# A chain of three products on one core: wider column blocks in the second product, and the norm's scale inside the hi/lo split of w_out

## The chip, the core and the metric

The kernel runs on one core of a Trainium2 chip. The core has five engines that run side by side: TensorE (PE, matmuls into PSUM), VectorE (DVE), ScalarE (ACT), GpSimd (POOL) and SyncE (SP, which only issues DMA transfers here). The metric is the device time of one execution in microseconds (us).

## What is computed

Attention with a soft cap, then two feed-forwards, all on 896 tokens. Cut to what matters:

```python
def _attn_ref(q, k, v, cap):          # 2 x 12 heads, 448 tokens, 64 wide
    scores = cap * np.tanh(scale * (q @ k.T) / cap)
    ...                                # softmax, times v
def _moe_ref(x, w_in, w_out, g_ln):    # x 896 x 768, w_in 768 x 1024, w_out 1024 x 768
    h = x @ w_in
    e = np.exp(h - h_max)
    solu = h * (e / (np.sum(e, axis=-1, keepdims=True) + 1e-09))
    ln = (solu - mu) / np.sqrt(var + 1e-06) * g_ln
    return ln @ w_out
def _moe2_ref(x, w_gate, w_val, w_out):  # 768 x 1536, 768 x 1536, 1536 x 768
    g = x @ w_gate
    return (g * (1.0 / (1.0 + np.exp(-g))) * (x @ w_val)) @ w_out
```

The weights of both feed-forwards are float64 in memory.

## The kernel before

**Numbers in two parts.** Every product of the feed-forwards is made of float32r parts: a value is split into hi (a copy in float32r) and lo (the value minus hi), and `mm3` adds three matmuls, hi x hi, hi x lo and lo x hi. A float64 weight comes in as a raw tile (`load64`, two buffers) and is made a float32 by `f32`: ScalarE takes the absolute value of the top words, VectorE clamps, shifts and then merges the sign and the low bits with two scalar_tensor_tensor operations on 512 columns (the "bit operations" below). Then ScalarE writes hi and VectorE lo.

**The stages.** Attention goes through 12 pairs of heads. The first feed-forward then goes through 7 tiles of 128 tokens. `ff1_h(t)` is 36 matmuls of 512 columns into two PSUM tiles and a tail of statistics: a maximum on VectorE, an exponential on ScalarE, sums, and the norm, whose last step (line 390) scales the tile `e_t`, on ScalarE for tiles 4 to 6 and on VectorE before. `ff1_T(t)` transposes `e_t` on PE (8 transposes, tiles `lt`) and splits it into hi and lo columns of l. The columns of the 896 tokens lie in three tiles: lA (384, tiles 0 to 2), lB (256, tiles 3 and 4) and lC (256, tiles 5 and 6, a part of the tile y).

**The second product.** w_out is taken in 6 column tiles of 128, `wo_j`, with three buffers. `load_w_out(j)` (line 417) makes each in two halves of 512 rows, that is 4 row blocks of 128 in each. The norm's g_ln is applied there: four ScalarE copies of 128 columns with a scale from a column of `gt`, in place (line 425), then one ScalarE copy of 512 for hi (line 426) and one VectorE subtraction of 512 for lo (line 427). `ff1_x2(j, ...)` is one column block of one output tile: for each of 8 row blocks the three matmuls of `mm3`, 24 in all, with wo_j as the weights and l as the moving columns. Its result is split into hi and lo again as x2, which the second feed-forward (`ff2_gv`, `ff2_out`) reads.

**What sets the order.** Up to line 541 the engines keep the order of the code. From there on a scheduler places the instructions of each engine by its own estimate of times, from the order of the code in the lists `steps` (lines 563 and 568): h[t], T[t], wo[j] and x2[j][n] are what `ff1_h`, `ff1_T`, `load_w_out` and `ff1_x2` put in. Parts marked as pinned keep the code's order also there: the first steps of `f32` in `load_w_out`. Each engine runs its own instructions strictly in the order in which they then stand.

Of the kernel before, what the change touches and what calls it, by code (L numbers as in the profile page):

```python
# [5 lines left out]
F32 = mybir.dt.float32  # L6
F32R = mybir.dt.float32r
U32 = mybir.dt.uint32
I64 = mybir.dt.int64
AF = mybir.ActivationFunctionType  # L10
ALU = mybir.AluOpType
# [25 lines left out]
class Kernel:  # L37
# [295 lines left out]
    def ff1_h(self, t):  # L333

        nc = self.nc
        st = {}

        def mm(kk):
            def go():
                if kk == 0:  # L340
                    if self.htag == "t":
                        ps = self.ph.tile([128, 2, 512], F32, name=f"h_{t}", tag="t")
                        st["h"] = [ps[:, f] for f in range(2)]
                    else:
                        st["h"] = [self.ph.tile([128, 512], F32, name=f"h_{t}_{f}", tag="m") for f in range(2)]
                a, z = kk == 0, kk == self.KD - 1
                xh, xl = self.xcols(t, kk)
                wh, wl = self.wi
                f = [slice(0, 512), slice(512, 1024)]
                for x, w, s, e in ((xh, wh, a, False), (xh, wl, False, False), (xl, wh, False, z)):  # L350
                    for i in range(2):
                        self.PE.matmul(st["h"][i], x, w[:, kk, f[i]], start=s, stop=e)
                if z:
                    tail()
            return go

        def tail():
            sm = self.slot("sm", [128, 32], f"sm_{t}", F32, bufs=3)
            e = self.slot("e", [128, self.F1], f"e_{t}", F32, bufs=2)
            h = st["h"]  # L360
            for f in range(2):
                self.V.tensor_reduce(sm[:, f:f + 1], h[f], axis=AX.X, op=ALU.max)
            self.V.tensor_scalar(sm[:, 2:3], sm[:, 0:1], sm[:, 1:2], -1.0, op0=ALU.max, op1=ALU.mult)
            for f in range(2):
                self.A.activation(e[:, f * 512:(f + 1) * 512], h[f], AF.Exp, bias=sm[:, 2:3],
                                     accum_out=sm[:, 3 + f:4 + f])
            self.V.tensor_scalar(sm[:, 5:6], sm[:, 3:4], sm[:, 4:5], 1e-9, op0=ALU.add, op1=ALU.add)
            self.V.reciprocal(sm[:, 6:7], sm[:, 5:6])

            sq = t >= 5  # L370
            for f in range(2):
                ef = e[:, f * 512:(f + 1) * 512]
                self.V.scalar_tensor_tensor(ef, ef, sm[:, 6:7], h[f], op0=ALU.mult, op1=ALU.mult,
                                               **({"accum_out": sm[:, 8 + f:9 + f]} if sq else {}))
                if not sq:
                    self.V.bn_stats(sm[:, 8 + 6 * f:14 + 6 * f], ef)
            if sq:
                r = self.F1 ** 0.5
                self.V.tensor_scalar(sm[:, 20:21], sm[:, 8:9], sm[:, 9:10], -1 / (self.F1 * r), op0=ALU.add, op1=ALU.mult)
                for f in range(2):  # L380
                    self.A.activation(h[f], e[:, f * 512:(f + 1) * 512], AF.Square, bias=sm[:, 20:21], scale=1 / r,
                                         accum_out=sm[:, 10 + f:11 + f])
                self.V.tensor_scalar(sm[:, 22:23], sm[:, 10:11], sm[:, 11:12], 1e-6, op0=ALU.add, op1=ALU.add)
            else:
                r = -1.0
                self.V.bn_aggr(sm[:, 20:22], sm[:, 8:20].rearrange("p (a s) -> p a s", s=6))
                self.V.tensor_scalar(sm[:, 22:23], sm[:, 21:22], 1e-6, None, op0=ALU.add)
            self.G.tensor_tensor(sm[:, 23:24], sm[:, 22:23], self.mhalf, op=ALU.pow)
            self.V.tensor_scalar(sm[:, 24:25], sm[:, 20:21], sm[:, 23:24], r, op0=ALU.mult, op1=ALU.mult)
            if t >= 4:  # L390
                self.A.activation(e, e, AF.Identity, bias=sm[:, 24:25], scale=sm[:, 23:24])
            else:
                self.V.tensor_scalar(e, e, sm[:, 23:24], sm[:, 24:25], op0=ALU.mult, op1=ALU.add)
            self.ln[t] = e

        return [(1.3, mm(kk)) for kk in range(self.KD)]
# [20 lines left out]
    def load_w_out(self, j):  # L417

        w = self.wos[j] = self.wo.tile([128, 2, self.K1, 128], F32R, name=f"wo_{j}", tag="wo")
        for i in range(2):  # L420
            c = slice(4 * i, 4 * i + 4)
            src = self.w_out[i * 512:(i + 1) * 512, j * 128:(j + 1) * 128].rearrange("(f p) d -> p f d", p=128)
            f = self.f32(self.load64(src, f"wo_{j}_{i}"), f"wo_{j}_{i}", pin=True).rearrange("p (f d) -> p f d", f=4)
            for m in range(4):
                self.A.activation(f[:, m], f[:, m], AF.Copy, scale=self.gt[:, 4 * i + m:4 * i + m + 1])
            self.hi_act(w[:, 0, c], f)
            self.lo_dve(w[:, 1, c], f, w[:, 0, c])

    def ff1_x2(self, j, get, N, o):

# [75 lines left out]
    def run(self):  # L506
        nc = self.nc
        KD, K1, K2, F1 = self.KD, self.K1, self.K2, self.F1
# [19 lines left out]
        w = [self.w_in_steps(i) for i in range(2 * KD)]  # L528
# [5 lines left out]
        h = [self.ff1_h(t) for t in range(7)]  # L534
# [12 lines left out]

        self.pt = self.ph = self.pool("pm", bufs=8, space=PSUM)
        self.htag, self.ttag = "m", "m"
        lA = self.slot("l", [128, K1, 2, 384], "lA")  # L550
        T = [self.ff1_T(t, lambda: lA, 128 * t) for t in range(3)]
        lp = self.pool("lp", side="right")
        self.wo = self.pool("wo", bufs=3, side="right")
        lB = lp.tile([128, K1, 2, 256], F32R, name="lB", tag="lB")
        self.y = self.slot("x", [128, KD * 2 * 896], "y")
        lC = self.y[:, :4096].rearrange("p (f u n) -> p f u n", f=K1, u=2)
        T3, T4 = self.ff1_T(3, lambda: lB, 0), self.ff1_T(4, lambda: lB, 128)
        T5, T6 = self.ff1_T(5, lambda: lC, 0), self.ff1_T(6, lambda: lC, 128)
        wo = [[(0.0, lambda j=j: self.load_w_out(j))] for j in range(KD)]
        blocks = ((lambda: lA, 384, 0), (lambda: lB, 256, 384), (lambda: lC, 256, 640))  # L560
        x2 = [[[self.ff1_x2(j, *blocks[n])] for n in range(3)] for j in range(KD)]

        steps = h[1] + T[0] + h[2] + T[1] + h[3][:2] + T[2] + h[3][2:] + h[4][:3] + wo[0] + h[4][3:] + wo[1] + h[5][:5] + T3 + h[5][5:] + h[6][:2] + T4 + h[6][2:]
        for _, f in steps:
            f()
        X = [self.slot(f"wi{u}", [128, 6144], f"x2_{u}") for u in range(2)]
        self.x2 = [X[j // 3][:, j % 3 * 1792:(j % 3 + 1) * 1792].rearrange("p (u n) -> p u n", u=2) for j in range(KD)]
        steps = x2[0][0] + x2[0][1] + wo[2] + x2[1][0] + T5 + x2[1][1] + T6 + x2[0][2] + x2[1][2]
        for j in range(2, KD):
            if j + 1 < KD:  # L570
                steps += wo[j + 1]
            if j >= KD - 2:
                steps += [(0.0, lambda i=j - KD + 2: self.load_gv(0, i))]
            steps += x2[j][0] + x2[j][1] + x2[j][2]
        for _, f in steps:
            f()
        self.wo.release()
# [1 line left out]


        ap = self.pool("ap", side="right")
        big = self.slot("l", [128, 6144], "a_0")
        ab = [big] + [ap.tile([128, 5376], F32R, name=f"a_{i}", tag=f"a_{i}") for i in range(1, 4)]
        w2x = self.y[:, :4608].rearrange("p (f u n) -> p f u n", f=6, u=2)
        for fc in range(K2):
            self.a[fc] = ab[fc // 3][:, fc % 3 * 1792:(fc % 3 + 1) * 1792].rearrange("p (u n) -> p u n", u=2)
        for fc in range(6):
            self.w2[0, fc] = w2x[:, fc]
        for i, t in enumerate([big] + X):
            self.w2[0, 6 + i] = t[:, 5376:].rearrange("p (u n) -> p u n", u=2)  # L590
        for fc in range(K2):
            for i, (N, o) in enumerate(((384, 0), (512, 384))):
                if fc + 1 < K2:
# [57 lines left out]
```

## Time and profile before

| | us |
|---|---|
| median of 3 runs | 509.64 (509.06 to 510.04) |
| the profiled execution | 509.66 |
| its span, first to last instruction | 507.9 |
| PE busy | 496.3 |
| VectorE busy | 348.0 |
| ScalarE busy | 256.7 |
| GpSimd busy | 20.7 |

The profiled execution's time is its span and some 1.8 us around it. A row of a timeline gives the start, the length, the engine, what is written and read, and how many instructions follow each other; in brackets stands idle time of the engine before it and what ended that. Lengths of instructions in a row overlap, since each engine begins the next before the last has left it; what one costs in a row is read from start to start.

### The profile page before, as it was taken

The numbers are of one execution on the slowest core, as the hardware profiler recorded it, in microseconds if no ns is written. First come the engines' busy times: TensorE is split into PE (matmuls) and PEld (weight loads), VectorE is DVE, ScalarE is ACT, GpSimd is POOL, SyncE is SP. The second block draws the span as 40 slices with busy tenths as digits, with TensorE's granted clock in tenths as the row PEclk, the third lists the DMA queues.
The fourth block names the chain that finished last, engine by engine and source line by source line (L and its number), as shares of the span: only waits on it lengthen the run. The fifth ranks groups of instructions, "written<-read, shape, count | busy, mean of one in ns | idle before, by whom it ended". The sixth has DMA issues, their size and how long they took to land.

```text
span 507.9 us, 7456 instructions
## 1 busy us (share of the span) xinstructions
PE 496.3 (98%) x2920; PEld 411.3 (81%) x2920; DVE 348.0 (69%) x625; ACT 256.7 (51%) x388; POOL 20.7 (4%) x63
## 2 busy tenths in 40 slices
PE   6999999999999999999999999999999999999996
PEld 5454444446788899999999988889999889999996
DVE  2788888873778895677899999897997868200000
ACT  2999999990313696474545454353444434100000
POOL 1111111110000000000000000000000000000000
PEclk8999999999999999999999999999999999999999
DMA  8955555320000222145354545435243525111111
GB/s 169 218 127 151 132 151 129 91 70 2 0 1 0 82 85 84 43 146 165 125 176 136 185 127 162 149 124 161 98 148 94 168 80 157 31 32 31 32 31 32
DMA packets 66916, 52.40 MB, mean 103 GB/s; under 512 B 35904, under 2 KB 62272, under 8 KB 66880
## 3 DMA queue, kind: packets, MB, share of 16 engines
q1 hardware_dynamic: 65184, 50.90, 35.5%
q10 hardware_dynamic: 1664, 1.02, 0.6%
q8 instruction: 23, 0.38, 0.3%
q14 instruction: 13, 0.11, 0.1%
q0 software_dynamic: 32, 0.00, 0.0%
HBM read 49.16 MB, written 2.75 MB: 102 GB/s over the span
## 4 chain that ended last, share of the span: by engine, by line
PE 93%; DMA 2%; ACT 2%; DVE 2%; issue 0%; ACTq 0%; POOL 0%; POOLq 0%
PE o L29 17%; PE g L29 17%; PE v L29 17%; PE x L29 10%; PE h L29 10%; PE pv L29 8%; PE sc L29 7%; PE S L29 4%; PE T L29 2%; DMA q<-in_q_dram 1%; PE lt L29 1%; DVE sm L29 1%; ACT P L29 1%; ACT wo L29 1%; DMA wo_raw<-in_moe_w_out_dram 1%; DVE e L29 0%
## 5 line engine op out<-in xcount | busy, mean ns | idle before, releaser
L29 PE MATMUL g<-x,y 128*128 128x512 f32 (+1 forms) x432 | 91.3, 363 | 0.0
L29 PE MATMUL v<-x,y 128*128 128x512 f32 (+1 forms) x432 | 90.5, 362 | 0.0
L29 PEld LDWEIGHTS g<-x,y 128*128 128x128 f32 x432 | 78.3, 188 | 8.8
L29 PEld LDWEIGHTS v<-x,y 128*128 128x128 f32 x432 | 78.2, 188 | 8.5
L29 PE MATMUL h<-wi,x 128*128 128x512 f32 x252 | 58.8, 392 | 0.0
L29 PEld LDWEIGHTS h<-wi,x 128*128 128x128 f32 x252 | 46.8, 188 | 10.9 <-issue 1.4
L29 PE MATMUL o<-x,a 128*128 128x384 f32 x294 | 52.4, 336 | 0.0
L29 PEld LDWEIGHTS o<-x,a 128*128 128x128 f32 x294 | 51.2, 188 | 0.0
L29 ACT ACTIVATE P<-sc,c 112x896 f32<-112x896 f32 x48 | 45.6, 999 | 3.1 <-PE sc L29 2.7
L29 ACT ACTIVATE P<-P,cp 112x1792 f32<-112x1792 f32 x24 | 43.1, 1795 | 0.5
L29 PE MATMUL pv<-P,v 112*64 112x448 f32 x192 | 41.2, 551 | 0.0
L29 PEld LDWEIGHTS sc<-ks 64*112 64x112 f32 x288 | 24.1, 176 | 19.6 <-issue 8.5
L493 ACT ACTIVATE ob<-o 128x384 f32<-128x384 f32 x14 | 6.9, 491 | 65.0 <-PE o L29 65.0
L29 PE MATMUL sc<-ks 64*112 64x448 f32 x288 | 36.8, 387 | 1.0 <-ACT P L29 1.0
L29 PE MATMUL o<-y,a 128*128 128x384 f32 x189 | 34.3, 337 | 0.0
L29 PEld LDWEIGHTS o<-y,a 128*128 128x128 f32 x189 | 33.2, 188 | 0.1
L29 PEld LDWEIGHTS pv<-P,v 112*64 112x64 f32 x192 | 11.7, 136 | 23.9 <-issue 16.6
L29 PE MATMUL x<-lA,wo 128*128 128x384 f32 x144 | 28.1, 337 | 0.9 <-ACT wo L29 0.9
L29 PEld LDWEIGHTS x<-lA,wo 128*128 128x128 f32 x144 | 24.3, 188 | 1.1 <-ACT wo L29 1.1
L29 ACT ACTIVATE a<-sg 128x384 fp32r<-128x384 f32 (+1 forms) x24 | 13.9, 578 | 21.9 <-DVE sg L469 21.8
L29 DVE SCALAR_TENSOR_TENSOR w<-w_raw,w 128x768 uint32<-128x768 uint32 (+1 forms) x26 | 23.1, 892 | 0.4
L29 ACT ACTIVATE wv<-wv_raw 128x768 f32<-128x768 f32 x12 | 10.9, 910 | 24.6 <-DMA wv_raw<-in_moe_w_val_dram 24.6
(97 smaller groups left out, 682.5 us busy)
## 6 DMA issues: line engine op xcount, KB each, us to landing
wg_raw<-in_moe_w_gate_dram SPq DMA_DIRECT2D x12, 768.0 KB, 4.3
wv_raw<-in_moe_w_val_dram SPq DMA_DIRECT2D x12, 768.0 KB, 4.3
w_raw<-in_moe_w_out_dram SPq DMA_DIRECT2D x11, 768.0 KB, 4.5
wi_raw<-in_moe_w_in_dram SPq DMA_DIRECT2D x12, 512.0 KB, 4.2
wo_raw<-in_moe_w_out_dram SPq DMA_DIRECT2D x12, 512.0 KB, 3.5
v<-in_v_dram SPq DMA_DIRECT2D x24, 112.0 KB, 2.8
k<-in_k_dram SPq DMA_DIRECT2D x23, 112.0 KB, 4.1
q<-in_q_dram SPq DMA_DIRECT2D x23, 112.0 KB, 4.6
```

The source lines that it names most:

```text
L29: i = f(*a, **k)
L493: nc.scalar.activation(ob, acc, AF.Copy)
```

## The change

Four things change, all from the first feed-forward's second product on.

- The columns of l lie in two tiles instead of three: lA has 512 (tiles 0 to 3), lB 384 (tiles 4 to 6), and lC is gone. `ff1_x2` then has two column blocks for each output tile. The orders of the lists `steps` are written anew: wo[0] to wo[2] stand before the end of the h stage, then come the first blocks of x2[0], x2[1] and x2[2] with T5 and T6 between them.
- In `load_w_out` the in-place scaling goes. ScalarE writes hi of each row block straight from the unscaled float32, with the scale; VectorE writes lo of each row block with one scalar_tensor_tensor of 128 columns, value times scale minus hi.
- The last step of the norm for tiles 4 and 5 is on VectorE instead of ScalarE.
- The tiles of the second feed-forward's a lie in three tiles instead of four.

```diff
-            if t >= 4:
+            if t >= 6:
                 self.A.activation(e, e, AF.Identity, bias=sm[:, 24:25], scale=sm[:, 23:24])
...
             for m in range(4):
-                self.A.activation(f[:, m], f[:, m], AF.Copy, scale=self.gt[:, 4 * i + m:4 * i + m + 1])
-            self.hi_act(w[:, 0, c], f)
-            self.lo_dve(w[:, 1, c], f, w[:, 0, c])
+                g, hi = self.gt[:, 4 * i + m:4 * i + m + 1], w[:, 0, 4 * i + m]
+                self.A.activation(hi, f[:, m], AF.Copy, scale=g)
+                self.V.scalar_tensor_tensor(w[:, 1, 4 * i + m], f[:, m], g, hi.bitcast(F32), op0=ALU.mult, op1=ALU.subtract)
...
-        lA = self.slot("l", [128, K1, 2, 384], "lA")
+        lA = self.slot("l", [128, K1, 2, 512], "lA")
...
-        lB = lp.tile([128, K1, 2, 256], F32R, name="lB", tag="lB")
+        lB = lp.tile([128, K1, 2, 384], F32R, name="lB", tag="lB")
...
-        lC = self.y[:, :4096].rearrange("p (f u n) -> p f u n", f=K1, u=2)
-        T3, T4 = self.ff1_T(3, lambda: lB, 0), self.ff1_T(4, lambda: lB, 128)
-        T5, T6 = self.ff1_T(5, lambda: lC, 0), self.ff1_T(6, lambda: lC, 128)
+        T3, T4 = self.ff1_T(3, lambda: lA, 384), self.ff1_T(4, lambda: lB, 0)
+        T5, T6 = self.ff1_T(5, lambda: lB, 128), self.ff1_T(6, lambda: lB, 256)
...
-        blocks = ((lambda: lA, 384, 0), (lambda: lB, 256, 384), (lambda: lC, 256, 640))
-        x2 = [[[self.ff1_x2(j, *blocks[n])] for n in range(3)] for j in range(KD)]
-
-        steps = h[1] + T[0] + h[2] + T[1] + h[3][:2] + T[2] + h[3][2:] + h[4][:3] + wo[0] + h[4][3:] + wo[1] + h[5][:5] + T3 + h[5][5:] + h[6][:2] + T4 + h[6][2:]
+        blocks = ((lambda: lA, 512, 0), (lambda: lB, 384, 512))
+        x2 = [[[self.ff1_x2(j, *blocks[n])] for n in range(2)] for j in range(KD)]
+
+        steps = h[1] + T[0] + h[2] + T[1] + h[3][:2] + T[2] + h[3][2:] + wo[0] + h[4][:3] + wo[1] + h[4][3:] + h[5][:2] + T3 + h[5][2:] + wo[2] + h[6][:2] + T4 + h[6][2:]
...
-        steps = x2[0][0] + x2[0][1] + wo[2] + x2[1][0] + T5 + x2[1][1] + T6 + x2[0][2] + x2[1][2]
-        for j in range(2, KD):
-            if j + 1 < KD:
-                steps += wo[j + 1]
-            if j >= KD - 2:
-                steps += [(0.0, lambda i=j - KD + 2: self.load_gv(0, i))]
-            steps += x2[j][0] + x2[j][1] + x2[j][2]
+        steps = x2[0][0] + x2[1][0] + T5 + x2[2][0] + T6
+        for j in range(3):
+            steps += x2[j][1] + wo[j + 3]
+        for j in range(3, KD):
+            if j > 3:
+                steps += [(0.0, lambda i=j - 4: self.load_gv(0, i))]
+            steps += x2[j][0] + x2[j][1]
...
-        big = self.slot("l", [128, 6144], "a_0")
-        ab = [big] + [ap.tile([128, 5376], F32R, name=f"a_{i}", tag=f"a_{i}") for i in range(1, 4)]
+        big = self.slot("l", [128, 8192], "a_0")
+        ab = [big] + [ap.tile([128, 7168], F32R, name=f"a_{i}", tag=f"a_{i}") for i in range(1, 3)]
```

On PE, behind the end of the h stage, before. In the names, `x2_1_0` is the PSUM tile of output tile 1 from column 0 on, `lt_5_0` the first transposes of token tile 5; the last number is a running one.

```order
L29 MATMUL lt_4_1_1798<-ident_100,e_4_1661 128x128 x4
L29 MATMUL x2_0_0_1849<-lA_1374,wo_0_1613 128x384 x14
L29 MATMUL x2_0_384_1876<-lB_1381,wo_0_1613 128x256
L29 MATMUL x2_0_0_1849<-lA_1374,wo_0_1613 128x384 x10
L29 MATMUL x2_0_384_1876<-lB_1381,wo_0_1613 128x256 x12
L29 MATMUL x2_1_0_1932<-lA_1374,wo_1_1678 128x384
L29 MATMUL x2_0_384_1876<-lB_1381,wo_0_1613 128x256 x11
L29 MATMUL x2_1_0_1932<-lA_1374,wo_1_1678 128x384 x11
L29 MATMUL lt_5_0_1959<-ident_100,e_5_1760 128x128 x4
```

The same place on PE now, as far as the first matmuls behind tile 6's transposes:

```order
L29 MATMUL lt_4_1_1839<-ident_100,e_4_1698 128x128 x4
L29 MATMUL x2_0_0_1890<-lA_1374,wo_0_1593 128x512 x24
L29 MATMUL x2_1_0_1917<-lA_1374,wo_1_1646 128x512 x5
L29 MATMUL lt_5_0_1944<-ident_100,e_5_1768 128x128 x4
L29 MATMUL lt_5_1_1951<-ident_100,e_5_1768 128x128 x4
L29 MATMUL x2_1_0_1917<-lA_1374,wo_1_1646 128x512 x19
L29 MATMUL x2_2_0_1958<-lA_1374,wo_2_1785 128x512 x2
L29 MATMUL lt_6_0_1985<-ident_100,e_6_1871 128x128 x4
L29 MATMUL lt_6_1_1992<-ident_100,e_6_1871 128x128 x4
L29 MATMUL x2_2_0_1958<-lA_1374,wo_2_1785 128x512 x10
```

Output tile 1 now stands behind the 24 matmuls of one block of output tile 0; before, all but one of its matmuls stood behind both blocks, 48. The second block of tile 0 has moved behind tile 6's transposes.

On VectorE, before, the last rows up to the second bit operation on wo_1's second half (`wo_1_1`; `wo_1_0` is the first half as float32, `sm_t` the statistics of token tile t):

```order
L29 TENSOR_TENSOR wo_1_1678<-wo_1_0_1681,wo_1_1678 128x512
L29 TENSOR_SCALAR sm_6_1829<-sm_6_1829 128x1
L29 TENSOR_SCALAR wo_1_1_1695<-wo_1_1_1695 128x512
L29 TENSOR_SCALAR sm_5_1759<-sm_5_1759 128x1
L29 TENSOR_SCALAR wo_1_1_1695<-wo_1_1_1695 128x512
L29 SCALAR_TENSOR_TENSOR wo_1_1_1695<-wo_1_1_raw_1693,wo_1_1_1695 128x512
L29 TENSOR_SCALAR sm_5_1759<-sm_5_1759 128x1
L29 TENSOR_SCALAR sm_6_1829<-sm_6_1829 128x1
L29 SCALAR_TENSOR_TENSOR wo_1_1_1695<-wo_1_1_raw_1693,wo_1_1_1695 128x512
```

And now, the last 12 of 31 instructions from the first maximum over tile 6's h to the same second bit operation:

```order
L29 SCALAR_TENSOR_TENSOR e_6_1871,sm_6_1870<-e_6_1871,sm_6_1870,h_6_1_1819 128x512
L29 TENSOR_TENSOR x2_0_1888<-x2_0_0_1890,x2_0_1888 128x512
L29 TENSOR_SCALAR wo_2_0_1788<-wo_2_0_1788 128x512
L29 TENSOR_SCALAR wo_1_1_1665<-wo_1_1_1665 128x512
L29 TENSOR_SCALAR sm_6_1870<-sm_6_1870 128x1
L29 TENSOR_TENSOR lB_1381<-lt_5_0_1944,lB_1381 128x4x128
L29 TENSOR_TENSOR lB_1381<-lt_5_1_1951,lB_1381 128x4x128
L29 TENSOR_SCALAR wo_2_0_1788<-wo_2_0_1788 128x512
L29 SCALAR_TENSOR_TENSOR wo_1_1_1665<-wo_1_1_raw_1663,wo_1_1_1665 128x512
L29 TENSOR_SCALAR sm_6_1870<-sm_6_1870 128x1
L29 SCALAR_TENSOR_TENSOR wo_2_0_1788<-wo_2_0_raw_1786,wo_2_0_1788 128x512
L29 SCALAR_TENSOR_TENSOR wo_1_1_1665<-wo_1_1_raw_1663,wo_1_1_1665 128x512
```

The 19 ahead of these are two maxima over h, two bit operations and one one-operand step on wo_1_0, one such step on wo_1_1, two subtractions into lB, four scalar_tensor_tensor of 128 columns into wo_1, tile 5's scaling (128x1024), one step with a sum on e_6, a reciprocal and four single-column steps. The second half of wo_1 now stands behind steps on wo_2 and behind tile 5's columns of lB, which came after it before.

## Rows read from the trace of the kernel before

**Rows 1.** The page, part 1: busy us (share of the span) and instructions by engine.

```profile
PE 496.3 (98%) x2920; PEld 411.3 (81%) x2920; DVE 348.0 (69%) x625; ACT 256.7 (51%) x388; POOL 20.7 (4%) x63
```

**Rows 2.** Stretch: length, busy us of PE, PEld, DVE, ACT, POOL; granted clock; DMA.

```profile
242.20:416.02 173.82, 173.82 (x867) 156.43 (x866) 152.64 (x237) 78.97 (x121) 0.00 (x0) 1.00 0.46 141
```

**Rows 3.** Timeline of PE, matmuls of three widths: start us, us, what.

```profile
222.61 2.25 PE L29 MATMUL x<-lA,wo 128*128 128x384 f32 x12
224.69 1.59 PE L29 MATMUL x<-lB,wo 128*128 128x256 f32 x12
226.12 1.54 PE L29 MATMUL x<-y,wo 128*128 128x256 f32 x12
227.50 0.51 PE L29 MATMUL x<-lA,wo 128*128 128x384 f32 x2
...
262.98 4.28 PE L29 MATMUL g<-x,y 128*128 128x512 f32 x18
267.10 4.24 PE L29 MATMUL v<-x,y 128*128 128x512 f32 x18
```

**Rows 4.** Timeline of PE: end of the h stage, and two waits.

```profile
179.10 1.03 PE L29 MATMUL lt<-ident,e 128*128 128x128 f32 x8
179.89 2.67 PE L29 MATMUL x<-lA,wo 128*128 128x384 f32 x14
...
194.91 1.03 PE L29 MATMUL lt<-ident,e 128*128 128x128 f32 x8
196.32 0.50 PE L29 MATMUL x<-y,wo 128*128 128x256 f32 x2 [0.37 <-ACT y L29]
...
215.41 1.31 PE L29 MATMUL x<-y,wo 128*128 128x256 f32 x10
217.60 0.61 PE L29 MATMUL x<-lA,wo 128*128 128x384 f32 x2 [0.88 <-ACT wo L29]
```

**Rows 5.** Timeline of VectorE behind h[6]: start us, us, what.

```profile
179.21 0.69 DVE L29 TENSOR_REDUCE sm<-h 128x1 f32<-128x512 f32 x1
179.81 0.68 DVE L29 TENSOR_TENSOR wo<-wo,wo 128x512 fp32r<-128x512 f32 x1
...
184.82 0.68 DVE L29 SCALAR_TENSOR_TENSOR wo<-wo_raw,wo 128x512 uint32<-128x512 uint32 x1
```

**Rows 6.** Groups by form, 130 to 245 us: count | busy us, mean ns | idle before.

```profile
L29 DVE SCALAR_TENSOR_TENSOR e<-e,sm,h 128x512 f32<-128x512 f32 x14 | 9.9, 744 | 0.2
...
L29 DVE TENSOR_SCALAR sm<-sm 128x1 f32<-128x1 f32 x28 | 5.4, 200 | 5.6 <-POOL sm L29 2.8 <-ACT e L29 2.6
L29 DVE TENSOR_SCALAR wo<-wo 128x512 f32<-128x512 f32 x12 | 5.1, 424 | 2.1 <-ACT wo L29 1.7
...
L29 DVE TENSOR_TENSOR x<-x,x 128x256 fp32r<-128x256 f32 x12 | 5.1, 422 | 4.2 <-ACT x L29 4.0
...
L29 DVE TENSOR_SCALAR e<-e,sm 128x1024 f32<-128x1024 f32 x4 | 3.3, 813 | 0.1
...
L29 DVE TENSOR_TENSOR lB<-lt,lB 128x512 fp32r<-128x512 f32 x4 | 2.7, 684 | 0.5 <-ACT lB L29 0.5
...
L29 ACT ACTIVATE wo<-wo,gt 128x128 f32<-128x128 f32 x48 | 15.4, 394 | 5.6 <-DVE wo L29 5.6
...
L29 ACT ACTIVATE e<-e,sm 128x1024 f32<-128x1024 f32 x3 | 3.7, 1247 | 3.2 <-DVE sm L29 3.2
```

**Rows 7.** Busy us by stretch, as in rows 2: the span's start and end.

```profile
5.40:7.70 2.30, 0.00 (x0) 0.00 (x0) 0.75 (x4) 0.51 (x1) 0.00 (x0) 1.00 1.14 257
7.80:9.00 1.20, 0.00 (x0) 0.00 (x0) 0.00 (x0) 0.00 (x0) 0.00 (x0) 0.50 1.37 169
9.00:14.50 5.50, 5.44 (x29) 4.24 (x30) 3.20 (x6) 2.42 (x3) 0.45 (x1) 0.50 0.96 206
...
503.90:506.00 2.10, 0.00 (x0) 0.00 (x0) 0.00 (x0) 0.49 (x1) 0.00 (x0) 1.00 0.29 86
506.10:507.90 1.80, 0.00 (x0) 0.00 (x0) 0.00 (x0) 0.00 (x0) 0.00 (x0) 0.50 0.01 3
```

More of the change, by code (lines that the diff above doesn't have):

```diff
@@ L581, in run @@
         ap = self.pool("ap", side="right")
-        big = self.slot("l", [128, 6144], "a_0")
-        ab = [big] + [ap.tile([128, 5376], F32R, name=f"a_{i}", tag=f"a_{i}") for i in range(1, 4)]
+        big = self.slot("l", [128, 8192], "a_0")
+        ab = [big] + [ap.tile([128, 7168], F32R, name=f"a_{i}", tag=f"a_{i}") for i in range(1, 3)]
         w2x = self.y[:, :4608].rearrange("p (f u n) -> p f u n", f=6, u=2)
         for fc in range(K2):
-            self.a[fc] = ab[fc // 3][:, fc % 3 * 1792:(fc % 3 + 1) * 1792].rearrange("p (u n) -> p u n", u=2)
+            self.a[fc] = ab[fc // 4][:, fc % 4 * 1792:(fc % 4 + 1) * 1792].rearrange("p (u n) -> p u n", u=2)
         for fc in range(6):
             self.w2[0, fc] = w2x[:, fc]
-        for i, t in enumerate([big] + X):
-            self.w2[0, 6 + i] = t[:, 5376:].rearrange("p (u n) -> p u n", u=2)
+        for i, t in enumerate([big[:, 7168:7936], X[0][:, 5376:], X[1][:, 5376:]]):
+            self.w2[0, 6 + i] = t.rearrange("p (u n) -> p u n", u=2)
         for fc in range(K2):
```

## The prediction

> **What bounds the kernel now.** I read the page first, then tables of busy time by stretch, then the timelines of PE and VectorE. TensorE is busy for 496.3 of the 507.9 us [rows 1], and in the second feed-forward for every one of 173.82 us [rows 2]. So the time is the length of one row of matmuls: it gets shorter only where a matmul gets cheaper or where PE stops waiting. I therefore ask two things of the change: what the same columns cost in other block widths, and which instruction PE waits for at each place where it may wait, before and after.
>
> **Matmuls in wider blocks.** The second product of the first feed-forward has 6 output tiles of 8 x 3 = 24 matmuls per column block: 432 matmuls in blocks of 384, 256 and 256, and 288 in blocks of 512 and 384. I take the price of one from start to start, since the durations overlap. Twelve of 384 columns take 224.69 - 222.61 = 2.08 us (173 ns each), twelve of 256 from lB 1.43 us (119 ns), twelve of 256 from y 1.38 us (115 ns); eighteen of 512 in the second feed-forward take 267.10 - 262.98 = 4.12 us (229 ns; the v group after them 227) [rows 3]. One of each width: 407 ns before, 400 to 402 ns after, so 144 x 6 or 7 ns: **1.0 us less**, 0.7 to 1.1. The columns are the same; only a fixed part of about 7 ns per matmul goes.
> The Trainium skill, page "TensorE: Matmul & The Clock Gate", section "Back-to-back issue gap", gives an isolated matmul N/2.4 + 2.5 ns. The trace disagrees with it for 512 columns (216 ns by the page, 227 to 229 here). By the page's formula, and this is an estimate, a dropped matmul saves 2.5 ns, the gain would be 0.4 us, and the sums below would each lie 0.6 us higher.
>
> **Waits that go.** PE has two holes in this stage. After the transposes of tile 6 it waits for the high half of lC (in y): 1.41 us from the 8 transposes to the next matmul, where the 8 after tile 4 need 0.79. Before the fourth output tile it waits for wo_3: 2.19 us from the start of 10 matmuls to the next, where 10 need 1.15 [rows 4]. Together 0.62 + 1.04 = **1.66 us**. In the changed order all six blocks of the first three output tiles stand before wo_3 is wanted, and 10 matmuls of x2[2] right behind tile 6's transposes, reading lA, which was full long before. I take both holes as gone.
>
> **The wait that comes.** In the new order PE reaches the second half of wo_1 much sooner in work, and VectorE reaches it much later. Both run from the same moment, the end of h[6].
> PE's side: 8 transposes of tile 4 (0.79 us), 24 matmuls of x2[0], 5 of x2[1], 8 transposes of tile 5 (0.79), 7 more of x2[1]; the thirteenth reads row block 4 of wo_1, from the second half. That is 36 x 0.227 + 2 x 0.79 = 9.8 us. Before, two blocks of x2[0] stood ahead of x2[1], and VectorE began the last bit operation on wo_1 184.82 - 179.10 = 5.7 us after h[6] [rows 4, 5].
> VectorE's side: in the new order 31 instructions stand from the first maximum over tile 6's h to the last bit operation on wo_1's second half. An instruction starts the next one some 0.09 us before its own end (0.69 us long, the next 0.60 us later [rows 5]). By that: 11 of 512 elements at 0.60, the last at its full 0.69; 5 one-operand steps on 512 (0.424 long [rows 6]) at 0.34; two of e with a sum at 0.66; tile 5's scaling of 1024, which came over from ScalarE, at 0.73; 7 single-column steps (0.20 long) at 0.11; and 4 of the new scale-and-subtract on 128 columns. No row shows that operation. Two-operand rows go by 0.131 us per 128 elements (0.422 for 256, 0.684 for 512), which gives 0.29; a scale from a column adds 0.06 (0.744 against 0.684) [rows 6]: 0.35 long, 0.26 apart. From below a single-column step bounds it (0.20 long), from above the 256-wide one with the column (0.48): 0.12 to 0.39 apart. I take 0.26, since both neighbours lie on one line. Sum: 6.60 + 0.69 + 1.70 + 1.32 + 0.73 + 0.77 + 1.04 = 12.9 us, from 0.1 us after h[6] [rows 4, 5]. Then ScalarE must write the high part of the block, 0.39 us [rows 6], before PE may go on: 13.4 us. Tile 6's statistics and the bit operations on wo_2's first half, which stand among these 31, are what was put before wo_1; nothing in the queue is free to wait.
> **PE stands still for 13.4 - 9.8 = 3.6 us**; I take 3.5, and 3.0 to 4.1 by the bounds of the new operation. After that ScalarE gives a row block of wo_1 at least each 0.39 us and PE needs 0.68 for its three matmuls, so there is one wait, not four. Queued behind the waiting matmul on PE is everything.
> Costed at nothing: ScalarE loses 12 copies of 512 and two scalings of 1024; that gives PE nothing while VectorE is the late one. Tile 4's scaling on VectorE is covered by h[6], 36 matmuls of 0.227 us. Tile 5's is the 13th of the 31, some 5.4 us after h[6], and its transposes come after 0.79 + 29 x 0.227 = 7.4 us; without those 2.0 us of cover its 0.73 us would show. From wo_3 on, each tile of w_out is converted behind 24 matmuls of 512 and 24 of 384 (9.6 us), and its VectorE work of 2 x (2 x 0.34 + 2 x 0.60 + 4 x 0.26) = 5.8 us fits. The loads of wo_0 to wo_2 stand earlier in the code, but SP issues the same transfers in the same order, each when its raw buffer has been read. The second feed-forward changes only in where its tiles lie.
> Sum without anything else: -1.0 - 1.66 + 3.5 = +0.84 us.
>
> **What the standstill does to the clock.** TensorE's granted clock is at its upper level (2.4 GHz, 1.00) through the second feed-forward [rows 2]. It fell to the lower (1.2 GHz, 0.50) twice. At the start PE did nothing from 5.4 us at the latest until 9.0; to 7.7 us the clock was 1.00, from 7.8 us it was 0.50, and it stayed there through 5.5 us in which PE worked again [rows 7]. At the end the last matmul ended at 503.9 us, the clock was 1.00 until 506.0 and 0.50 from 506.1 on [rows 7]. So it fell some 2.3 and 2.2 us into an idle stretch, and the new standstill is longer than either. The holes of before, 1.0 us and less, never took it. That it falls here in every execution the two rows don't prove; I give it two chances in three. Its price: at half the rate the work done in the slow stretch takes twice as long, so half of 5.5 us is lost if as much follows as at the start, 2.75 us, and nothing if it doesn't fall. I take **1.6 us**, a little over the middle, since here 512-column matmuls follow at once where at the start short ones and waits did.
> The Trainium skill, the same page, section "Why this matters for your kernels", says to leave no long idle gap between bursts of matmuls, since the clock then goes back to half. By that rule the fall is certain rather than likely, and the sum is that of my forecast.
>
> **The forecast.** The profiled execution took 509.66 us for its span of 507.9, and the median of the runs is 509.64, so changes in the span are added to 509.65. Forecast: 509.65 + 0.84 + 1.6 = **512.1 us**, by itself 511.0 to 513.6.
>
> **The rivals.**
> 1. *The same standstill, and the clock stays up.* For it: two falls are few, and both came beside idle engines. 509.65 + 0.84 = 510.5 us, 510.0 to 511.2 by the new operation's bounds: at the edge of what can be told from no change.
> 2. *The standstill is short, and the wider blocks and closed holes show.* It would need VectorE to finish wo_1 some 2.5 us sooner than its 31 instructions add up to. Against it: in this stretch of before it runs back to back, and their order is fixed. Even then tile 6 is late next: its last statistic stands right behind those 31, and its scaling on ScalarE is 1.25 us long [rows 6], which leaves up to 1 us of waiting. It gives 509.65 - 2.66 + 0 to 1.0 = 507.0 to 508.0; above that it runs into the first rival. It decides in its own favour once the new wait is under 1.6 us.
> 3. *The hole moves on.* wo_2's second half comes late as well, as it is converted behind wo_1: another 1 us or a longer slow stretch, 513.6 and more. Against it: after the standstill PE has two dozen matmuls of x2[1] and x2[2] before it needs that half.
>
> **How the numbers follow.** Forecast 0.52, first rival 0.30, second 0.15, third 0.03. What a measurement of this kernel can tell from no change is about 0.2%, 1.0 us: 508.6 to 510.7. The first rival lies in it for 0.21 of its 0.30 and above it for 0.09; of the second, 0.12 lie below 508.6 and 0.03 inside. Faster 0.12, same 0.24, slower 0.52 + 0.09 + 0.03 = 0.64. The range leaves out the second rival and the third: 509.6 to 513.6.
>
> **What the changed profile would show.** Right: 288 matmuls of x2 at 227 and 173 ns from start to start; no wait on y or wo_3; one PE wait of some 3.5 us in x2[1] at about 189 us, put down to ScalarE's wo with VectorE busy without a hole before it; and behind it a stretch with the granted clock at 0.50. Wrong: a PE wait there under 2 us, or matmuls of 512 columns at more than 235 ns at full clock; the new VectorE operation outside 0.20 to 0.48 us; a wait of over 0.5 us at wo_2 to wo_5; or a clock that stays at 1.00 through the standstill, which turns the forecast into the first rival.

## The result and the profile after

The changed kernel takes **512.59 us** (median of 14 runs, 511.09 to 515.53) against 509.50 for the kernel before on the same chip (14 runs): ratio **1.0069**, 95% interval 1.0054 to 1.0084. The forecast was 512.1 in 509.6 to 513.6. The profiled execution took 512.51 us for a span of 510.7.

The page, part 1, answers to [rows 1]: 1.5 us more of PE busy time with 144 matmuls fewer, and 5.8 us more on VectorE.

```profile
PE 497.8 (97%) x2776; PEld 405.5 (79%) x2776; DVE 353.8 (69%) x657; ACT 246.8 (48%) x368; POOL 21.7 (4%) x63
```

The timeline of PE from tile 4's transposes to the second feed-forward answers to [rows 3, 4]: start us, length, what is written and read, count, and in brackets idle time and what ended it.

```profile
178.18 1.04 PE L29 MATMUL lt<-ident,e 128*128 128x128 f32 x8
178.97 6.90 PE L29 MATMUL x<-lA,wo 128*128 128x512 f32 x29
185.71 1.03 PE L29 MATMUL lt<-ident,e 128*128 128x128 f32 x8
186.50 1.85 PE L29 MATMUL x<-lA,wo 128*128 128x512 f32 x7
191.50 0.73 PE L29 MATMUL x<-lA,wo 128*128 128x512 f32 x2 [3.15 <-ACT wo L29]
192.59 4.62 PE L29 MATMUL x<-lA,wo 128*128 128x512 f32 x12 [0.35 <-DVE wo L29]
197.04 1.03 PE L29 MATMUL lt<-ident,e 128*128 128x128 f32 x8
...
201.21 2.77 PE L29 MATMUL x<-lB,wo 128*128 128x384 f32 x15
203.81 2.46 PE L29 MATMUL x<-lA,wo 128*128 128x512 f32 x10
206.11 9.18 PE L29 MATMUL x<-lB,wo 128*128 128x384 f32 x52
...
244.65 3.31 PE L29 MATMUL g<-x,y 128*128 128x384 f32 x18
```

Read the starts. Tile 4's transposes to the first g: 244.65 - 178.18 = 66.47 us, before 242.20 - 179.10 = 63.10. So **3.4 us come in this stage**. PE does 7 matmuls from 186.50 and is at the next one only at 191.50: 5.00 us where 7 need 1.6. Two matmuls on, it waits once more, this time for VectorE. Then 12 matmuls take 197.04 - 192.59 = 4.45 us, 371 ns each instead of 230: that is the slow clock. The table by stretch (length, busy us and count of PE, PEld, DVE, ACT, POOL, granted clock, DMA share, GB/s) shows it, and the second feed-forward beside it, which answers to [rows 2]:

```profile
193.53:196.94 3.41, 3.41 (x10) 2.60 (x9) 2.48 (x7) 2.21 (x6) 0.00 (x0) 0.50 0.69 206
244.65:418.27 173.62, 173.62 (x865) 156.25 (x865) 151.97 (x236) 78.29 (x121) 0.00 (x0) 1.00 0.45 140
```

The list of PE's waits over this stage has two entries only. None names y, and none wo_3:

```profile
PE x L29 <- ACT wo L29: 3.1, 1, 3.1
PE x L29 <- DVE wo L29: 0.4, 1, 0.4
```

VectorE's timeline behind h[6] answers to [rows 5], and two groups by form to [rows 6]; the second fence gives count, busy us, mean ns of one, idle time before.

```profile
178.15 0.69 DVE L29 TENSOR_REDUCE sm<-h 128x1 f32<-128x512 f32 x1 [0.54 <-PE h L29]
...
182.84 0.81 DVE L29 TENSOR_SCALAR e<-e,sm 128x1024 f32<-128x1024 f32 x1
183.56 0.16 DVE L29 RECIPROCAL sm<-sm 128x1 f32<-128x1 f32 x1
183.63 0.86 DVE L29 SCALAR_TENSOR_TENSOR wo<-wo,gt,wo 128x128 fp32r<-128x128 f32 x3
184.41 0.74 DVE L29 SCALAR_TENSOR_TENSOR e<-e,sm,h 128x512 f32<-128x512 f32 x1
...
189.73 1.28 DVE L29 SCALAR_TENSOR_TENSOR wo<-wo_raw,wo 128x512 uint32<-128x512 uint32 x2
191.46 0.21 DVE L29 TENSOR_SCALAR sm<-sm 128x1 f32<-128x1 f32 x1 [0.44 <-POOL sm L29]
191.59 0.68 DVE L29 SCALAR_TENSOR_TENSOR wo<-wo_raw,wo 128x512 uint32<-128x512 uint32 x1
192.19 1.14 DVE L29 SCALAR_TENSOR_TENSOR wo<-wo,gt,wo 128x128 fp32r<-128x128 f32 x4
```

```profile
L29 ACT ACTIVATE wo<-wo,gt 128x128 fp32r<-128x128 f32 x48 | 15.3, 392 | 8.9 <-DVE wo L29 8.9
L29 DVE SCALAR_TENSOR_TENSOR wo<-wo,gt,wo 128x128 fp32r<-128x128 f32 x48 | 14.4, 347 | 1.4 <-ACT wo L29 1.4
```

From 178.15 to the end of the last bit operation on wo_1 (189.73 + 1.28 = 191.01) VectorE works without a gap. ScalarE's hi row blocks begin at 191.05, having waited for it, and PE goes on at 191.50. ScalarE's timeline:

```profile
191.05 1.28 ACT L29 ACTIVATE wo<-wo,gt 128x128 fp32r<-128x128 f32 x4 [1.93 <-DVE wo L29]
```

The lo row blocks, at 192.19, stand behind a statistic that waits 0.44 us for GpSimd and behind a bit operation on wo_2: this is the second wait.

Outside this stage two things differ. PE is at tile 4's transposes 0.92 us earlier. This comes from the start, which the edit doesn't touch: PE waits 2.19 us for the first q instead of 3.73, and the slow clock there lasts 3.41 us instead of 6.83. And the last 252 matmuls take 0.45 us longer; the timelines of PE, of the kernel before and of the changed one:

```profile
459.84 44.03 PE L29 MATMUL o<-x,a 128*128 128x384 f32 x252
```

```profile
462.24 44.48 PE L29 MATMUL o<-x,a 128*128 128x384 f32 x252
```

3.37 - 0.92 + 0.45 - 0.04 (the gate and value products) = 2.86 us, and the profiled executions differ by 512.51 - 509.66 = 2.85.

### The profile page after: what moved, and what is told of

Read it like the earlier page. It is cut to its first block, busy times and chain, and to the rows that moved or that the text cites. A ratio compares the mean times of both kernels' runs of the same rounds, so it can differ in the third digit from the quotient of the medians.

```text
span 510.7 us, 7184 instructions
## 1 busy us (share of the span) xinstructions
PE 497.8 (97%) x2776; PEld 405.5 (79%) x2776; DVE 353.8 (69%) x657; ACT 246.8 (48%) x368; POOL 21.7 (4%) x63
## 3 DMA queue, kind: packets, MB, share of 16 engines
HBM read 49.16 MB, written 2.75 MB: 102 GB/s over the span
## 4 chain that ended last, share of the span: by engine, by line
PE 92%; DVE 3%; DMA 2%; issue 1%; ACT 0%; POOLq 0%; ACTq 0%; POOL 0%; SPq 0%; DVEq 0%
PE o L29 17%; PE g L29 17%; PE v L29 17%; PE x L29 10%; PE h L29 10%; PE pv L29 8%; PE sc L29 7%; PE S L29 4%; DMA q<-in_q_dram 2%; PE T L29 2%; DVE sm L29 1%; PE lt L29 1%; DVE wo L29 1%; DVE e L29 1%; DVE lB L29 0%
## 5 line engine op out<-in xcount | busy, mean ns | idle before, releaser
L29 PE MATMUL x<-lA,wo 128*128 128x512 f32 x144 | 38.1, 409 | 3.5 <-ACT wo L29 3.1
L29 PEld LDWEIGHTS x<-lA,wo 128*128 128x128 f32 x144 | 27.5, 195 | 9.4 <-ACT wo L29 3.6
L29 PE MATMUL x<-lB,wo 128*128 128x384 f32 x144 | 27.4, 335 | 0.0
L29 PEld LDWEIGHTS x<-lB,wo 128*128 128x128 f32 x144 | 25.4, 188 | 1.2
```

The costliest lines, as they stand in the source:

```text
L29: i = f(*a, **k)
```

## Experiments

**Is the clock really paid for?** My theory: of the loss, some 1.7 us are the slow clock, and the rest is the standstill. The rival: the 512-column matmuls behind the wait are slow for another reason, such as lo row blocks that arrive late. Two kernels keep the changed one and its wait, and give PE useless matmuls of 512 columns into a PSUM tile that nobody reads, 13 or 7 of them, in the place where it would stand. For this x2[1]'s first block is cut in two, and PE keeps the code's order in the second part.

```diff
+                spare = self.pt.tile([128, 512], F32, name="spare", tag="m")
+                for _ in range(n):
+                    self.PE.matmul(spare, w[:, 0, 3, :], l[:, 3, 0, :], start=True, stop=True)
                 for fc in range(4, 8):
```

> The changed kernel with 13 matmuls of 512 columns more on TensorE, into a PSUM tile that nobody reads, placed behind tile 5's transposes and before the second half of x2[1]; VectorE's order up to wo_1 is the changed kernel's. They take 13 x 0.227 = 2.95 of the 3.4 to 3.8 us in which PE stands still, so PE arrives at the same moment but has worked. If the slow clock behind the standstill is due to the standstill: clock at 1.00 behind it, about 1.7 us less than the changed kernel, 510.8 us. If it comes from something else (the 512-column blocks, the load of all engines): no gain, 512.6 us, and half clock at the same place.

> The same with 7 such matmuls (1.6 us), which leaves some 2.0 us of standstill in one piece. Standstill theory: between the two, 510.8 to 512.6 us, with the clock falling in fewer of the executions than in the changed kernel. If the fall has another cause: 512.6 us.

With 13: 510.72 us, ratio 1.0038 (1.0027 to 1.0050), as the first theory has it. PE's timeline, and busy time and granted clock of PE over the stretch:

```profile
178.78 1.03 PE L29 MATMUL lt<-ident,e 128*128 128x128 f32 x8
...
189.93 1.99 PE L29 MATMUL spare<-lA,wo 128*128 128x512 f32 x8
192.10 0.73 PE L29 MATMUL x<-lA,wo 128*128 128x512 f32 x2 [0.18 <-ACT wo L29]
193.18 3.03 PE L29 MATMUL x<-lA,wo 128*128 128x512 f32 x12 [0.35 <-DVE wo L29]
196.05 1.03 PE L29 MATMUL lt<-ident,e 128*128 128x128 f32 x8
...
243.56 3.31 PE L29 MATMUL g<-x,y 128*128 128x384 f32 x18
```

```profile
188.00:204.00 16.00, 15.47 (x78) 1.00 0.33 100
```

The same 12 matmuls now take 2.87 us instead of 4.45 us, though the wait for lo ahead of them is the same 0.35 us; the clock stays at 1.00. The stage is 243.56 - 178.78 = 64.78 us long, 1.69 less than in the changed kernel (66.47), with useless work in the place of the hole. So the clock's price is shown: 1.7 us, half of the slow stretch of 3.41.

With 7: 511.44 us, ratio 1.0052 (1.0037 to 1.0067). In the profiled execution the wait for hi was 1.55 us and that for lo 0.35, the clock fell all the same, again for 3.41 us, and the stage was as long as in the changed kernel (66.45).

```profile
192.92:196.33 3.41, 3.41 (x10) 2.67 (x9) 2.76 (x7) 2.09 (x7) 0.00 (x0) 0.50 0.72 205
```

A profile is one execution, but the mean granted clock of every execution is on record. One of the six with 7 useless matmuls, the one that took 510.48 us, has 1.000: there the clock did not fall at all. The span times one minus the mean clock is 4.0 us on average over the 14 executions of the changed kernel and 2.2 over 50 of the kernel before. The 1.8 us more are what about one such stretch in each execution would give. This is an estimate, and the scatter is wide: the six with 13 and the six with 7 both give 3.0.

**Which part of the change brings the standstill?** Theory: VectorE's row behind h[6], whatever lengthens it. One part is undone at a time, or done alone. Undone alone: the norm of tiles 4 and 5 (`oldnorm`), the new split (`oldsplit`). Done alone: the wide blocks (`blocks`, both of these undone, but with the new orders of the lists and the new places of a), the split (`splitonly`, in the kernel before).

```diff
# oldnorm, in the changed kernel
-            if t >= 6:
+            if t >= 4:
# oldsplit, in the changed kernel; splitonly is its reverse in the kernel before
-                self.A.activation(hi, f[:, m], AF.Copy, scale=g)
-                self.V.scalar_tensor_tensor(w[:, 1, 4 * i + m], f[:, m], g, hi.bitcast(F32), op0=ALU.mult, op1=ALU.subtract)
+                self.A.activation(f[:, m], f[:, m], AF.Copy, scale=self.gt[:, 4 * i + m:4 * i + m + 1])
+            self.hi_act(w[:, 0, c], f)
+            self.lo_dve(w[:, 1, c], f, w[:, 0, c])
```

> The changed kernel with one part undone: the scaling of tiles 4 and 5 is on ScalarE again. 0.73 us less in VectorE's row before wo_1, and the scheduler places wo_1's steps anew: the wait breaks into two of about 1.0 and 1.2 us with one row block between them. Theory of the order: about 1.2 us less waiting than the changed kernel, and the clock stays up in some executions: 509.3 to 511.3 us. Rival, the new split alone is the cause: no more than the 0.7 us of VectorE work, 511.9 us.

> The changed kernel with the w_out split undone: four scaled copies in place, one copy and one subtraction of 512. VectorE does 0.44 us less for each half of a wo tile, ScalarE 0.53 more. If the new 128-column operation is the cause: the standstill shrinks by 0.9 us or more and the time falls to 510 or below. Theory of the order: the scheduler places the rows anew and another wait comes in at wo_2, so it is no better, 511.5 to 513.5 us, with waits of about 2.7 us at x2[1] and 1.3 at x2[2].

> The wider blocks alone: the w_out split and the place of the norm's scaling as before the change. Theory of the order: the blocks bring wo_1 closer to the end of the h stage, and that alone makes the standstill; two waits of about 1.6 and 2.8 us at x2[1], the clock falls, 512.7 to 514.7 us. If the other two parts make it: 507 to 508.5 us.

> The kernel before with only the w_out split changed: blocks of 384, 256 and 256, and the order of the list as they were. If the new split were neutral: 509.5 us. Theory of the order: its 0.44 us more for each half push back tile 5's and tile 6's rows on VectorE, so that PE waits about 2.5 us for each of the two (at tile 5's transposes and for lC); 513 us, and 515 where the clock falls.

| kernel | us | ratio to before (95%) | PE's waits in the stage | clock in the profiled execution |
|---|---|---|---|---|
| changed | 512.59 | 1.0069 (1.0054 to 1.0084) | 3.1 + 0.4 | fell at 193.53 |
| oldnorm | 510.61 | 1.0025 (1.0012 to 1.0038) | 0.8 + 0.9 | fell at 192.08 |
| oldsplit | 511.74 | 1.0054 (1.0037 to 1.0071) | 2.6 | fell at 192.75 |
| blocks | 513.10 | 1.0078 (1.0064 to 1.0092) | 2.4 + 1.3 | stayed at 1.00 |
| splitonly | 512.77 | 1.0070 (1.0053 to 1.0087) | 2.3 + 2.3 | fell at 200.45 |

The stretch of slow clock in `oldnorm`, in the columns of the table by stretch:

```profile
192.08:195.49 3.41, 3.41 (x11) 2.62 (x10) 3.08 (x9) 1.54 (x5) 0.00 (x0) 0.50 0.50 154
```

The lists of PE's waits (us in total, times, longest) of `oldnorm`, `blocks` and `splitonly`:

```profile
PE x L29 <- DVE wo L29: 0.9, 1, 0.9
PE x L29 <- ACT wo L29: 0.8, 1, 0.8
```

```profile
PE x L29 <- ACT wo L29: 3.7, 2, 2.4
```

```profile
PE lt L29 <- ACT e L29: 2.3, 1, 2.3
PE x L29 <- ACT y L29: 2.3, 1, 2.3
```

The blocks with their new order alone cost as much as everything together, and so does the split alone, each by making PE wait for what VectorE and ScalarE have yet to finish, but at different places: wo_1 with the new blocks, tiles 5 and 6 with the old ones. So the parts do not add up. But the theory of VectorE's row alone is too narrow, as `blocks` shows at its longer wait:

```profile
189.45 0.68 DVE L29 SCALAR_TENSOR_TENSOR wo<-wo_raw,wo 128x512 uint32<-128x512 uint32 x1
190.47 1.27 ACT L29 ACTIVATE wo<-wo,gt 128x128 f32<-128x128 f32 x4
191.64 1.24 ACT L29 ACTIVATE e<-e,sm 128x1024 f32<-128x1024 f32 x1
192.77 0.62 ACT L29 ACTIVATE wo<-wo 128x512 fp32r<-128x512 f32 x1
193.44 3.81 PE L29 MATMUL x<-lA,wo 128*128 128x512 f32 x14 [2.39 <-ACT wo L29]
```

VectorE has done its bit operations by 190.13; then ScalarE's own row, without a gap and with tile 6's scaling in it, keeps hi until 193.39, and PE goes on at 193.44. The old split puts four scalings and a copy on ScalarE ahead of hi; with the new one, in the changed kernel, PE goes on 0.5 us after VectorE's last bit operation (191.01 to 191.50). Of the parts undone, the norm's move brought the most: with the scaling of tiles 4 and 5 back on ScalarE, and the scheduler's placing that follows from it, the waits fall by half. `oldsplit` came out in its range and with the first wait as expected, but the second one, at x2[2], did not come: a miss. In `blocks` the clock stayed up through two waits in the profiled execution, where I expected a fall, and two shorter ones in `oldnorm` were followed by one; that the time of `blocks` lies in its range is thus no support for what I said of its clock. Another of the 12 executions of `oldnorm` has a mean clock of 1.000, so its waits are not followed by a fall each time.

**Is it the order, then?** If the rows are too long only behind h[6], converting w_out earlier must bring the gain of the wide blocks out. `wo_order` moves nothing but the places of wo[0], wo[1] and wo[2] in the list of steps; `best` has its own places for them and the norm of tiles 4 and 5 on ScalarE again.

```diff
# in both: where wo[0], wo[1], wo[2] stand in the list
-  T[2] + h[3][2:] + wo[0] + h[4][:3] + wo[1] + h[4][3:] + ... + h[5][2:] + wo[2] + h[6][:2] + T4 + h[6][2:]
+  T[2] + wo[0] + h[3][2:] + wo[1] + h[4][:3] + h[4][3:] + ... + h[6][:2] + T4 + wo[2] + h[6][2:]      # wo_order
+  T[2] + wo[0] + h[3][2:] + h[4][:3] + wo[1] + h[4][3:] + ... + h[6][:2] + wo[2] + T4 + h[6][2:]      # best
# in best alone
-            if t >= 6:
+            if t >= 4:
```

> The changed kernel with the three loads of w_out at other places of the list of steps and nothing else: wo[0] before the last four of h[3], wo[1] right behind them, wo[2] behind T4. All three parts of the change stay. If the place at which VectorE reaches wo_1 makes the standstill: no wait of over 0.6 us in x2, some 1.3 us of waits in three pieces in all, clock at 1.00, about 508.5 us. If the new 128-column operation is what costs (48 of them, 14 us of VectorE): standstill as before, 512 us.

> The changed kernel with wo[0] before the last four of h[3], wo[2] before T4, and the scaling of tiles 4 and 5 back on ScalarE. VectorE then has 0.73 us less in front of wo_1. Theory of the order: no wait of PE from tile 4's transposes to the second feed-forward; 1.66 us of old waits and 0.5 to 1.0 us of matmuls less than before: 506.8 to 507.6 us, faster than both. Rival, that wider blocks bring nothing of their own and the old waits only move: 508.5 to 509.5 us.

`wo_order`: 508.48 us, ratio 0.9990 (0.9976 to 1.0004), the waits 0.4 and 0.3. `best`: **507.19 us, ratio 0.9965** (0.9953 to 0.9977), faster than both kernels. PE's timeline in `best`, and its table over 62 us:

```profile
178.79 1.04 PE L29 MATMUL lt<-ident,e 128*128 128x128 f32 x8
179.58 11.25 PE L29 MATMUL x<-lA,wo 128*128 128x512 f32 x48
190.66 1.03 PE L29 MATMUL lt<-ident,e 128*128 128x128 f32 x8
...
239.57 3.31 PE L29 MATMUL g<-x,y 128*128 128x384 f32 x18
```

```profile
178.00:240.00 62.00, 62.00 (x320) 55.62 (x319) 48.09 (x113) 33.72 (x79) 1.41 (x2) 1.00 0.30 98
```

PE is busy for all of it. The stage takes 239.57 - 178.79 = 60.78 us, 2.3 less than before: the two old waits (1.66) and 0.5 to 0.7 from the wider blocks. So those gains were there. `wo_order` shows that the order had cost them, and more: with all parts of the change in place, new places in the list take some 4 us off. The last 1.3 us to `best` come from its other places and the norm on ScalarE together; no run tells these two apart.

**Where do the 0.45 us at the end come from?** The 252 matmuls of the second half take 44.48 us in the changed kernel and in every kernel made from it so far, 44.03 in `splitonly`. Their forms, their number and their moving columns (w_out2, in X) are the same. Two things were moved by the edit: the PSUM banks in which these products stand (6 tiles fewer are taken ahead of them), and the place of one of the twelve tiles of a, the fourth; the other eleven lie where they lay. Both kernels are made from `best`.

```diff
# banks
+        for i in range(6):
+            self.V.memset(self.pt.tile([128, 512], F32, name=f"skip_{i}", tag="m")[:, :1], 0.0)
         for half in range(2):
# a_place
-            self.a[fc] = ab[fc // 4][:, fc % 4 * 1792:(fc % 4 + 1) * 1792].rearrange(...)
+            self.a[fc] = (big[:, 6256:8048] if fc == 3 else ab[fc // 4][:, fc % 4 * 1792:(fc % 4 + 1) * 1792]).rearrange(...)
-        for i, t in enumerate([big[:, 7168:7936], ...]):
+        for i, t in enumerate([big[:, 5376:6144], ...]):
```

> The version with the early w_out and the norm on ScalarE, with six PSUM tiles taken and left unused ahead of the second feed-forward's output products, so that these stand in the same PSUM banks as before the change. In every kernel with the new blocks the output products of the second feed-forward took some 0.43 us longer than before (88.1 us against 87.7, the second half's matmuls 176 ns apart against 173). Theory A, the banks: with them back in place the stage takes 87.7 us and the time falls by 0.4 us to about 506.8. Theory B, something else (the places of a, or what the trace does not show): the stage stays at 88.1 us and the time at 507.2. The six one-column writes on VectorE stand ahead of the stage, where VectorE waits, and cost nothing by either.

> The version with the early w_out and the norm on ScalarE, with one of the twelve tiles of a (the fourth) moved 3520 bytes up within its buffer, and the w_out tile that stood behind it put where it stood before the change. The fourth tile of a is the only one whose place the change moved. Theory A, the place of that tile slows the second feed-forward's output products: the stage, 88.1 us from its first matmul to its last in every kernel with the new blocks against 87.7 before, changes by more than 0.1 us, towards 87.7 if the new place is as good as the old. Theory B, something that the trace does not show: the stage stays at 88.1 us and the time at 507.2.

`banks`: 507.18 us, and the row stays at 44.48. `a_place`: **506.56 us, ratio 0.9953** (0.9936 to 0.9969), the lowest time of all, though its interval overlaps that of `best`. What decides is the row, which is that of the kernel before again; `banks` first, then `a_place`:

```profile
457.01 44.48 PE L29 MATMUL o<-x,a 128*128 128x384 f32 x252
```

```profile
456.67 44.03 PE L29 MATMUL o<-x,a 128*128 128x384 f32 x252
```

The small w_out2 tile that moved along is read in the first half only, whose length is 43.96 to 43.98 us in all of these kernels. So it is the place of the fourth tile of a in SBUF (`a_place` gives it a third place, not the one of before). From start to start the 252 matmuls are 175.9 ns apart on average instead of 174.1. Those of ten of the twelve tiles were slower, not those that read this tile alone; why that is, and which places are bad, stays open.

## Why the prediction was right

By its own steps:

- **Matmuls in wider blocks, -1.0 us: right in sign, too large.** 384 columns cost (203.81 - 201.21) / 15 = 173 ns, as taken. 512 columns cost (206.11 - 203.81) / 10 = 230 ns, where I took 227 to 229 from the second feed-forward. One of each is 403 instead of 407 ns, so 144 x 3.7 ns = 0.5 us. The failing step: 2 ns on a small difference of large numbers.
- **Waits that go, -1.66 us: right.** No wait on y or wo_3 is left, and `best` shows the gain.
- **The wait that comes, +3.5 us: right in place, cause and size of the first wait, short by the second.** VectorE needs 191.01 - 178.15 = 12.9 us for its 31 instructions (12.9 forecast). The 128-column operation is 347 ns long (0.35) and 0.26 apart (three from 183.63 to 184.41). PE goes on 13.3 us behind h[6] (13.4) and loses 5.00 - 1.61 = 3.4 us. What I left out is that the third matmul of `mm3` wants lo, not hi. I let PE go on as soon as ScalarE had written hi; lo stood on VectorE behind a statistic waiting for GpSimd and a bit operation: another 0.6 us (1.09 from 191.50 to 192.59, where two matmuls need 0.46). The standstill was 4.0 us by the starts. `wo_order` shows the cause: with the same operations, and only the loads of w_out at other places, the wait there is 0.4 us.
- **The clock, +1.6 us: right, 1.7.** `fill13` shows it: half of the slow stretch is lost, as forecast. That the stretch would be 3.41 us long, and not 5.5 as at the start, I had not foreseen; the 1.6, a choice between 0 and 2.75, came this near by luck. My reading of where it falls was less good: it fell at 193.53, when PE had worked again for 2 us, not during the idle time as in [rows 7], and not behind every wait (`blocks`). One profiled execution doesn't test the two chances in three; the mean clocks of the 14 fit a fall in most of them. The Trainium skill, page "TensorE: Matmul & The Clock Gate", section "Why this matters for your kernels", asks for no long idle gaps between bursts of matmuls. The changed kernel agrees, with a gap of 3.15 us and the fall behind it; in `oldnorm` two waits under 1 us each had a fall of the same length behind them, so short ones can have it too.
- **"The second feed-forward changes only in where its tiles lie", costed at nothing: wrong.** The place of one tile was worth 0.45 us.

The terms by the rows: -0.5 - 1.66 + 4.0 + 1.7 = 3.5 us against 3.37 in the stage. The too large gain of the blocks, the second wait and the place of a make the forecast some 1.4 us too low, all three the same way. It lies only 0.5 us below the measured 512.59, and that is in part luck: the profiled execution began 0.9 us earlier than the one of before, and against the medians of these runs, 3.1 us apart, the forecast of 2.4 is 0.7 short. In the later comparisons the kernel before took 508.75 to 509.24 us, not 509.50, so the true cost may lie nearer to the 3.8 us of the rows. The third rival (a further wait at wo_2) did not come. The first, the same standstill without the fall, is what `fill13` imitates: 510.7 against 510.5 forecast. The second, no standstill and the gains showing, did not come either; `best`, another kernel, shows what it would have given: 507.2, in its 507.0 to 508.0.

## What to carry to other kernels

Where PE is never idle, a change that makes matmuls cheaper also makes PE arrive earlier at its weights: add up the rows of the engines that make them, from a common start, down to the last part that the matmul reads (lo as well as hi), before counting the gain. If a row is too long, move the conversions ahead of the moment at which the race begins, before moving work between engines. When tiles get new places, compare matmuls that the edit did not touch, row by row.

## What the hardware showed that was not expected

- The place of one SBUF tile of weights changed the pace of a whole run of matmuls from 174.1 to 175.9 ns on average, repeatably: the 252 matmuls took 44.48 us in the changed kernel, `best` and `banks`, 44.03 in the kernel before and `a_place`. Another PSUM bank changed nothing.
- The granted clock fell to 0.50 after PE had taken up work again, in the changed kernel some 5.4 us after its idle time began (188.1 to 193.53), and for 3.41 us in each of the five profiled executions that had a fall in this stage. Two waits of 0.8 and 0.9 us were followed by a fall in one kernel; two of 2.4 and 1.3 us in another were not. What decides is not settled by these runs.
